# Local and strided attention with a gated feed-forward: scale and identity in the first mask's load, zeros in the values of three units, ScalarE for the last half tile

## The chip, the cores and the metric

One core of a Trainium2 chip. The time is the device time of one execution in microseconds (us); the profile's times count from the first instruction of the profiled execution. PE is TensorE, DVE VectorE, ACT ScalarE, POOL GpSimd, SP SyncE, which issues most DMAs; P V is the product of the attention weights with the values.

## The reference

```python
scores = scale * np.matmul(q, k.transpose(0, 1, 3, 2))        # 8 batches, 8 heads, 576 rows, 64 wide
mask_local = (rel >= 0) & (rel < 32)                          # heads 0 to 3
mask_strided = (rel >= 0) & (pos[None, :] % 32 == pos[:, None] % 32)   # heads 4 to 7
scores = np.where(masks, scores, -1e9); attn = softmax(scores)
x = matmul(attn, v).transpose(0, 2, 1, 3).reshape(4608, 512)
xn = x / sqrt(mean(x * x) + 1e-6) * rms_g                     # the norm, rms_g is its scale
g = xn @ w_gate; val = xn @ w_val                             # 512 x 1536
out = (silu(g) * val) @ w_out                                 # 1536 x 512
```

## The kernel before, in words

Attention is cut into 32 units, one batch and two heads each (numbered from 0; units 0 and 1 of a batch are local heads, 2 and 3 strided ones; the host has put strided heads' rows in residue order, so both kinds are bands). A unit's scores are nine blocks of 64 keys for two halves and two heads. For units 0 to 7 PE first adds the mask by a product with the identity (L744), then the blocks' scores (L759), 36 products of 64 rows by 32 columns. For units 1 to 3 (`PADDED`) the host puts zeros between the two heads in q, so that one product of 128 rows by 64 columns does both heads: 18 products, and q is twice as large. DVE reduces the maxima (L768), ACT takes the exponential (L794, nine small instructions with their sums; for units 2 and 3 PE first subtracts the maximum, L776, and ACT does one pass, L780), DVE divides and transposes, and PE multiplies with the values (L859), 40 products of 32 rows by 64 columns in fp32.

The 4608 tokens are nine chunks of 512. Chunk 0 goes alone: its blocks are squared (L927), summed over rows by PE (L936), scaled by the norm's scale and split into a high and a low part for fp32r products (`convert0`, ACT L992 and DVE L993), then multiplied with the gate and value weights (L1154 and L1164, three products of 128 x 128 x 512 for each block), while the weights, loaded as 64-bit words by SP (L1062), are turned into high and low parts by ACT (L1061, L1066) and DVE (L1069, L625, L1031) and written back to DRAM. The other eight chunks go in pairs by a scheme with seven products for eight (L1308, L1461), with the weights' parts loaded again; the remaining units' attention is set between them.

The order on every engine is made by a planner, `Plan`: each operation is recorded with engine, cost and what it reads and writes; then `forward` places them by a table of due numbers (`DUE`) and some holds. `PLACE` says which of 94 SBUF slots of 128 x 512 each buffer gets, tile names `bl`. So the program's order is fixed before it runs; only semaphores hold an engine. In the opening `LOADS` gives the order of SP's loads: q and k, constants (c0 near mask, c1 strided mask, c2 identity and scale on ACT's queue), v, first weights (w). Four units run in the opening, with filler products on a zero tile (L644) where PE would stand still. At the end each half of the last output tiles is copied from PSUM by ACT and DVE (256 columns each, L623 and L625), and stored (L1549).

Of the kernel before, what the change touches and what calls it, by code (L numbers as in the profile page):

```python
# [25 lines left out]
P = 128  # L26
# [7 lines left out]
MIX = 20  # L34
SWAP = 20
FREE = 5
# [11 lines left out]
NCST = 4 * SW + P  # L48
# [5 lines left out]
PADDED = (1, 2, 3)  # L54
# [21 lines left out]
LOADS = ('q0','c2','c0','q1','c1','q2','v0','q3','v1','w','v2','v3')  # L76
# [7 lines left out]
TLEAD = 2  # L84
PEM = (2,3)
# [9 lines left out]
    "0806003218102404140c0e2c0a5434424f300a003d4d5339221c2152225c55344d3a563e5a282e32001426340818120830202c0a181c1002223b433a"  # L95
    "1400241a5037414b45283032040c2220184636384c5d1c261206593c493b3f142e2c1a28080a044446184a400c00101847504c45481c323006143402"
    "1a5d3b4b5b57282422144e3a44574c0c262c041c2e2006580c0d5d401f4c4a4b1f132a505104342235005859504f032b443f2a145341154338002940"
    "3a3b493139023047584e284c55161a040816060c104842014a563e4b2725191e1f1832484a4d51545237425a1b3746181c205c243e363c264a242c06"
    "143410242d324254164807233d19561a2e085a3e5c461c17013c4a1e04320c244b15193e143352513c0a4d5134205a1c5c17190b070c010e421c322c"
    "1024563c151d07215c4a3d1f2e08523c1504072513154b213c562c340c245a20423533054d0a4a225c321021093415340a223d204d2e240c2c0c4a5a"  # L100
    "4a0d2e420152234b522f2e344442032d3f0813413c215c2700594e2b3d0b25523b120a43243a2a0239580e314c100c0d34402c44473f090f50115513"
    "414f423c532724260149120e432a223d405c004458300825390b2921342d09383c543a53525a38554e41100a4759133e4f483f2831433b51204b3731"
    "23420e00282b0c5c30220d2a11274903434d1e011f1d02561c400844533c5229500f322647355825410b0a3d0959543824395a514c3b12363a10454e"
    "5d5b2146344f485518153e1705421b1a3c431e5306071a1b04401d4d500c144f1d20105517003c1e442f4832233428451f5d13313f4b5515554e575c"
    "42160f3410060e483252533c1946231e375313342b202d1f453a3235293e0157531642574b1a1640452d04075c4d43462b4537054431561e465b293f"
    "1050463e0252080f434b3e5c16501c370e3e1f562350282135483f1a19455318421b133f2035293e460f1f3f081f401e37430e48564d1d4618071b43"
# [12 lines left out]
    "22092354380406580834034e5d365a3f4b43481d0c4c213a3c2911533e2b05072f2c500b3d4f4e0459103135095d254928572a27265b55303248060e"
    "583e0503002b0d2e3c4c0113460f421251194a0402244e390a07385453200c223f362d475d2f5808214b515a433c233a4c051d1924"))  # L120
DUE = np.frombuffer(bytes.fromhex(
    "005a02f60c5a01f801880d2401b30004004e002f03870da7000501a900010000000901f0000600020040025000280035001b0019003700230036001e"
    "001d006c011500aa0122005f00af02c000d100690dac003d0022001a0039002c006601240007012e0d9a024c011d013300da017800a20053004f0101"
    "003b001800030008000a0538009a00b10038004c00120da200a600b5011b01c80da9011402b8009e008e008c0105005c0044004300290011000f01e2"
    "01a605cb0206026504fa0015017e00a401e001a0017c01b6011201e401db007400f9011a01160106010400ef01e5024f00e101d600b000d9014e0263"
    "016102cd01460421025d00bf00e400ad01f700ca00e201d70401034200bd02f400b300c1014c017a022b02de02a2017500e001540266032d02560317"
    "03000319051401e103c401c9025c040f00fe008500ba006200c5007f0076019d002e028402010197017d01dc01d5016b01bf01c30179021b006b02f2"
    "01760237013501ac029301ba023a030102a802430279008100550024002b02f302ec03100153020301ea02180100012b019500b2014501b401be03ee"
    "020f007c00750292015a01eb000b0016000d030b00f5010800bc01e902260264021c01c4029702b7029801c201d30325000c010f014100e301d00152"
    "00d70194025f031c023b01a40182009401cd01a70177018a027d00d601d2007100be039e02e9037402cc021f02fb02e700f20285027c01af016f017f"  # L130
    "00f4013400e9030401df01cc016201bb01fa025902bc028d023100bb00b701cf011e0213032e009f012700c8012f00fa009c006000970367034f0323"
    "010e013e01020186028e028702df02e60163021901a5012c014d019b00d0009b0031001c000e038a019c010d0189023800cf02ba01a201c502d100f7"
    "03320308015101f6033b01e60014008001c1033801a302db023f01f2025502ae02520242020e010c02c1029c01710290026e032a02d3023d022c0283"
    "032002ed039c045003f603bf00d400ed009d015c0086018c004802b202cb026b025800990198010b019102ca02e002e502d90061023902a30267045f"
    "01ad02340343013f028c026d02d0031e0187024d057e021103f2022f016d02c40371027f02270348014401a80275007d022a02720020007e00100235"
    "02dd02320262037a026901650202018f02a70303021d02f001aa0280033c02d202eb02d70251027703e2031502f8026802d502a6035b022d01c00220"
# [332 lines left out]
def attn_moe(ctx: ExitStack, tc: tile.TileContext, qz: bass.AP, qT: bass.AP, kT: bass.AP, vz: bass.AP, vl: bass.AP,  # L469
# [209 lines left out]
    def load_consts(n):  # L679
# [5 lines left out]
        if n != 2:  # L685
            return
# [1028 lines left out]
```

## Time and profile before

| | |
|---|---|
| timed runs | 910.35, 913.11, 917.94 us (median 913.11) |
| the profiled execution | 909.69 us |
| its span, first to last instruction | 907.9 us |
| PE / DVE / ACT busy | 890.1 / 713.0 / 540.3 us |
| DMA, mean over the span | 256 GB/s |

The page divides the span by engine and by line; a group of instructions has its busy time, the mean time of one, and what ended the idle time before it. Matmuls are pipelined, so their records overlap. A released wait is put down to the last semaphore; "issue" means that the profile shows nothing that the engine waited for.

### The profile page before, as it was taken

The numbers are of one execution on the slowest core, as the hardware profiler recorded it, in microseconds if no ns is written. First come the engines' busy times: TensorE is split into PE (matmuls) and PEld (weight loads), VectorE is DVE, ScalarE is ACT, GpSimd is POOL, SyncE is SP. The second block draws the span as 40 slices with busy tenths as digits, with TensorE's granted clock in tenths as the row PEclk, the third lists the DMA queues.
The fourth block names the chain that finished last, engine by engine and source line by source line (L and its number), as shares of the span: only waits on it lengthen the run. The fifth ranks groups of instructions, "written<-read, shape, count | busy, mean of one in ns | idle before, by whom it ended". The sixth has DMA issues, their size and how long they took to land.

```text
span 907.9 us, 21329 instructions
## 1 busy us (share of the span) xinstructions
PE 890.1 (98%) x8570; PEld 718.4 (79%) x8574; DVE 713.0 (79%) x1204; ACT 540.3 (60%) x1154; POOL 1.7 (0%) x14
## 2 busy tenths in 40 slices
PE   7999999999999999999999999999999999999998
PEld 5677788777787877887887888888888888888886
DVE  5889999999888999566779998555699973357972
ACT  5899886688678694455538663444458533334520
POOL 0000000000000000000000000000000000000000
PEclk9999999999999999999999999999999999999999
DMA  9999997999787839957656669655364797353822
GB/s 342 353 411 410 392 414 277 402 410 387 259 318 268 300 116 339 336 165 234 196 175 205 201 204 388 236 157 172 124 206 159 251 359 266 105 163 94 287 97 79
DMA packets 104899, 232.81 MB, mean 256 GB/s; under 512 B 11616, under 2 KB 13920, under 8 KB 102496
## 3 DMA queue, kind: packets, MB, share of 16 engines
q1 hardware_dynamic: 104080, 230.86, 72.5%
q8 instruction: 67, 1.10, 0.5%
q10 hardware_dynamic: 720, 0.59, 0.2%
q14 instruction: 32, 0.26, 0.1%
HBM read 179.51 MB, written 51.90 MB: 255 GB/s over the span
## 4 chain that ended last, share of the span: by engine, by line
PE 85%; DVE 7%; ACT 3%; DMA 3%; issue 2%; ACTq 0%; DVEq 0%
PE a L1308 21%; PE v L1308 13%; PE g L1308 13%; PE a L1461 10%; PE g L1461 6%; PE v L1461 6%; PE a L1209 3%; PE g L1154 3%; PE v L1154 3%; PE pair L750 2%; DVE bl L631 2%; PE pair L846 2%; DMA bl<-gvd 1%; DVE bl L1264 1%; PE a L846 1%
## 5 line engine op out<-in xcount | busy, mean ns | idle before, releaser
L1308 PE MATMUL a<-bl,bl 128*128 128x512 f32 x850 | 215.4, 394 | 0.6 <-DMA bl<-gvd 0.6
L1308 PEld LDWEIGHTS a<-bl,bl 128*128 128x128 f32 x850 | 157.0, 188 | 35.2 <-DVE bl L1481 1.0
L623 ACT CAST bl<-bl 128x512 fp32r<-128x512 f32 (+1 forms) x214 | 130.3, 645 | 75.0 <-DVE bl L1264 24.7
L631 DVE TENSOR_TENSOR bl<-bl,bl 128x512 fp32r<-128x512 f32 x244 | 159.4, 684 | 7.2 <-ACT bl L623 2.7
L1308 PE MATMUL v<-bl,bl 128*128 128x512 f32 x563 | 145.3, 391 | 0.3 <-ACT bl L1316 0.3
L1308 PE MATMUL g<-bl,bl 128*128 128x512 f32 x562 | 144.7, 390 | 0.3 <-DVE bl L1346 0.3
L1264 DVE TENSOR_TENSOR bl<-bl,bl 128x512 f32<-128x512 f32 x169 | 114.0, 684 | 33.7 <-ACT bl L1325 30.7
L1308 PEld LDWEIGHTS v<-bl,bl 128*128 128x128 f32 x563 | 105.2, 188 | 23.9 <-DVE bl L1346 1.1
L1308 PEld LDWEIGHTS g<-bl,bl 128*128 128x128 f32 x562 | 105.1, 188 | 23.1 <-DVE bl L1346 0.8
L1320 DVE TENSOR_TENSOR a<-a,bl 128x512 f32<-128x512 f32 x96 | 66.8, 696 | 70.8 <-PE a L1308 60.4
L1461 PE MATMUL a<-bl,bl 128*128 128x512 f32 x422 | 99.2, 391 | 0.3 <-DVE bl L631 0.3
L1461 PEld LDWEIGHTS a<-bl,bl 128*128 128x128 f32 x422 | 78.9, 188 | 17.3 <-DVE bl L631 0.7
L1461 PE MATMUL g<-bl,bl 128*128 128x512 f32 x279 | 66.9, 390 | 0.0
L1461 PE MATMUL v<-bl,bl 128*128 128x512 f32 x279 | 66.5, 389 | 0.0
L1461 PEld LDWEIGHTS g<-bl,bl 128*128 128x128 f32 x279 | 52.2, 188 | 11.1
L1461 PEld LDWEIGHTS v<-bl,bl 128*128 128x128 f32 x279 | 52.4, 188 | 10.9
L1316 ACT COPY bl<-v 128x512 f32<-128x512 f32 x48 | 28.2, 588 | 50.9 <-PE v L1308 48.3
L1316 ACT COPY bl<-g 128x512 f32<-128x512 f32 x48 | 28.3, 589 | 48.5 <-PE g L1308 48.5
L1325 ACT ACTIVATE bl<-a 128x512 f32<-128x512 f32 x48 | 28.7, 601 | 46.8 <-DVE a L1320 46.7
L1031 DVE TENSOR_TENSOR bl<-bl,bl 128x512 fp32r<-128x512 f32 (+1 forms) x54 | 45.7, 859 | 1.0 <-ACT bl L623 0.9
L1316 ACT COPY bl<-a 128x512 f32<-128x512 f32 x48 | 28.2, 588 | 25.3 <-PE a L1308 22.6
L625 DVE CAST bl<-bl 128x512 fp32r<-128x512 f32 (+1 forms) x84 | 36.5, 444 | 6.8 <-PE v L1308 3.4
(175 smaller groups left out, 1161.2 us busy)
## 6 DMA issues: line engine op xcount, KB each, us to landing
bl<-gvd SPq DMA_DIRECT2D x288, 256.0 KB, 4.6
bl<-od SPq DMA_DIRECT2D x168, 256.0 KB, 3.7
gvd<-bl SPq DMA_DIRECT2D x12, 1024.0 KB, 9.0
bl<-in_wgv_dram SPq DMA_DIRECT2D x11, 1024.0 KB, 11.6
wd<-bl SPq DMA_DIRECT2D x18, 512.0 KB, 9.5
bl<-wd SPq DMA_DIRECT2D x18, 512.0 KB, 7.9
vt<-in_vl_dram SPq DMA_DIRECT2D x24, 352.0 KB, 5.4
xq<-in_qT_dram SPq DMA_DIRECT2D x28, 288.0 KB, 6.3
```

What stands on the lines that cost most here:

```text
L623: nc.scalar.copy(out=o, in_=i)
L625: nc.vector.tensor_copy(out=o, in_=i)
L631: elementwise(CH, lambda e: both(e).tensor_tensor(out=lo.new(F32R), in0=src(), in1=hi.f32(), op=ALU.subtract), reads + [hi.key], [lo.key])
L846: nc.tensor.matmul(out=ends[r % 2][0][n][64 * h:64 * h + 64, at + 32 * lo:at + 32 * hi], lhsT=va()[32 * r:32 * r + 32, D * (6 * n + j):D * ...
L1031: elementwise(len(l) * 256, lambda e, l=l, zs=zs: both(e).tensor_tensor(out=sides(l, 1, F32R), in0=cols(zs), in1=sides(l, 0), op=ALU.subtr ...
L1154: nc.tensor.matmul(out=out_, lhsT=q.t[:, w + at:w + at + P], rhs=x.t, start=(kc == 0 and i == 0), stop=(kc == KC - 1 and i == 2))
L1264: elementwise(CH, lambda e: both(e).tensor_tensor(out=o.new() if fresh else o.t, in0=a.t, in1=b.t, op=how), [a.key, b.key], [o.key])
L1308: nc.tensor.matmul(out=banks[bk], lhsT=w, rhs=xs[k][y].t, start=start and k == 0 and i == 0, stop=stop and k == 1 and i == 2, skip_group_c ...
L1316: op("ACT", act(CH, True), 0, lambda: nc.scalar.copy(out=t.new(), in_=banks[bk]), reads=[bk], writes=[t.key])
L1320: op("DVE", dve(CH), 0, lambda: nc.vector.tensor_tensor(out=banks[bk], in0=banks[bk], in1=t.t, op=ALU.add), reads=[t.key], writes=[bk])
L1325: op("ACT", act(CH, True), 0, lambda: nc.scalar.activation(out=t.new(), in_=banks[bk], func=AF.Silu), reads=[bk], writes=[t.key], tab="silu")
L1461: nc.tensor.matmul(out=banks[bks[j]], lhsT=v, rhs=xs[k][y].t, start=start and k == 0 and i == 0, stop=stop and k == KT - 1 and i == 2, ski ...
```

## The change

- The near mask, the identity and the norm's scale lie side by side in the constants, and one load of SP (c0, 356 words a partition) brings them; the two loads on ACT's queue go. `identb` and `gt` are views of the mask tile `cb`. c0 comes before c2, which is now only the copy of the identity to fp32 on ACT.
- `PADDED` is empty: units 1 to 3 load q once, and take 36 products for their scores.
- `PADV` holds units 1 to 3: the host lays out their values with zeros, twice as large (`vw`), and one product of 64 rows by 128 columns does both heads: 20 products for P V.
- In the last tile's second half both copies are ACT's; the first is stored by SP, the second by ACT.
- `DUE`, `PLACE` and a hold have new values, so the order on all engines and all slots are new. Loads, products and conversions are otherwise the same in number. In the part with the pairs of chunks PE's order stays.

```diff
-PADDED = (1, 2, 3)
+PADDED = ()
-LOADS = ('q0','c2','c0','q1','c1','q2','v0','q3','v1','w','v2','v3')
+LOADS = ('q0','c0','c2','q1','c1','q2','v0','q3','v1','w','v2','v3')
+PADV = (1,2,3)
+PVW = 1350.0
...
-    "0806003218102404140c0e2c0a5434424f300a003d4d5339221c2152225c55344d3a563e5a282e32001426340818120830202c0a181c1002223b433a"
+    "0c321c00081410242006301a563c394b3d0e322843184748222038595840515b27113f4a531c22203408320c2e1412282c180a102e1c162c24393a36"
...
-HOLD_A = [25.0, 0.0, 150.0, 50.0]
+HOLD_A = [25.0,0.0,100.0,50.0]
...
-    cb = sbt([P, 2 * SW], "cb", BF16)
-    identb = sbt([P, P], "identb", BF16)
+    cb = sbt([P, 2 * SW + P + 2 * KC], "cb", BF16)
+    identb = cb[:, 2 * SW:2 * SW + P]
...
-    gt, rcol = few[:, 0:4], few[:, 12:16]
+    gt, rcol = cb[:, 2 * SW + P:].bitcast(F32), few[:, 12:16]
...
-    homes = [(group(4), take2()) for _ in range(NPRO)]
+    homes = [(group(4), group(4) if i in PADV else take2()) for i in range(NPRO)]
...
-        if n == 3:
-            op("SP", 430, 0, lambda: nc.sync.dma_start(out=cb, in_=consts[:, 2 * SW + P:]), writes=["cb", "cb1"], bytes_=P * SW * 4)
-        elif n < 2:
-            op("SP", 430, 0, lambda: nc.sync.dma_start(out=cb[:, SW * n:SW * n + SW], in_=consts[:, SW * n:SW * n + SW]),
-               writes=["cb" + "1" * n], bytes_=P * SW * 2, follow="SP")
+        a, e = ((SW, 2 * SW + P + 2 * KC), (0, SW), (), (0, 2 * SW))[n] or (0, 0)
         if n != 2:
+            at = (n == 3) * (2 * SW + P + 2 * KC)
+            op("SP", 430, 0, lambda: nc.sync.dma_start(out=cb[:, a:e].bitcast(F32), in_=consts[:, (at + a) // 2:(at + e) // 2]), writes=(["cb", "identb", "gt"], ["cb1"], [], ["cb", "cb1"])[n],
+               bytes_=P * (e - a) * 2, run=(1424, 1152, 0, 2304)[n], follow="SP" if n < 3 else None)
             return
-        op("ACT", 430, 0, lambda: nc.scalar.dma_start(out=identb, in_=consts[:, 2 * SW:2 * SW + P]), writes=["identb"], bytes_=P * P * 2, follow="ACT")
-        op("ACT", 430, 0, lambda: nc.scalar.dma_start(out=gt, in_=gain), writes=["gt"], bytes_=2048, follow="ACT")
...
-        n = D * (NBL + 1 if i < EIGHT else NVB)
+        n = D * (NBL + 1 if i < EIGHT else NVB) * (1 + (i in PADV))
...
-        op("SP", 430, 0, lambda: nc.sync.dma_start(out=va(), in_=vz[i] if i < EIGHT else vl[i - EIGHT]), writes=[kv], bytes_=P * n * 4, rel=REL.get(i, 0.0), follow="SP" if pro else None)
+        op("SP", 430, 0, lambda: nc.sync.dma_start(out=va().rearrange("p (a n) -> p a n", a=2), in_=vw[PADV.index(i)].rearrange("a p n -> p a n")) if i in PADV else
+           nc.sync.dma_start(out=va(), in_=vz[i] if i < EIGHT else vl[i - EIGHT]), writes=[kv], bytes_=P * n * 4, run=2560 if i in PADV else 2048, rel=REL.get(i, 0.0), follow="SP" if pro else None)
...
                     for s in range(2):
-                        for h in range(2):
+                        keys = slice(64 * kb - 32 * (kb > 0), min(64 * kb + 32, SW))
+                        if i in PADV:
+                            r = slice(64 * s, 64 * s + 64)
+                            nc.tensor.matmul(out=pr[s][:, 32 * lo:32 * hi], lhsT=va()[r, P * kb:P * kb + P], rhs=pT[r, keys],
+                                             start=kb == 1, stop=kb == NBL - 1, skip_group_check=True)
+                        for h in range(0 if i in PADV else 2):
                             r = 32 * (2 * s + h)
...
-            for n, (e, q) in enumerate((("ACT", nc.scalar), ("DVE", nc.sync))):
+            for n, (e, q) in enumerate((("ACT", nc.scalar), ("DVE", nc.sync)) if more or not j else (("ACT", nc.sync), ("ACT", nc.scalar))):
...
+    vw = np.zeros((max(len(PADV), 1), P, NBL + 1, 2, D), vz.dtype)
+    for n, i in enumerate(PADV):
+        for h in range(2):
+            of = part[part // 32 % 2 == h]
+            vw[n, of, :, h] = vz[i, of].reshape(-1, NBL + 1, D)
```

PE, opening: from the end of unit 0's scores. Before, with `a_85`, `a_86` the banks of unit 1 and `identb` the identity, unit 1's scores:

```order
L744 LDWEIGHTS identb
L744 MATMUL a_85<-cb,identb 128x320
L744 LDWEIGHTS identb
L744 MATMUL a_86<-cb,identb 128x256
L759 MATMUL a_85<-bl_133 64x64 x10
L759 MATMUL a_86<-bl_133 64x64 x8
```

After, two units (line 761 is 759 of before; fillers stand ahead of this piece instead of between the units):

```order
L746 LDWEIGHTS cb
L746 MATMUL a_84<-cb 128x320
L746 LDWEIGHTS cb
L746 MATMUL a_85<-cb 128x256
L761 MATMUL a_84<-bl_137 32x64 x20
L761 MATMUL a_85<-bl_137 32x64 x16
L746 LDWEIGHTS cb
L746 MATMUL a_86<-cb 128x320
L746 LDWEIGHTS cb
L746 MATMUL a_87<-cb 128x256
L761 MATMUL a_86<-bl_145 32x64 x20
L761 MATMUL a_87<-bl_145 32x64 x16
```

Unit 1 and unit 2 have 36 products each now, and follow one another directly.

ACT, opening: before, from unit 1's exponentials, the exponentials of unit 2 (780), the first half weight (1061, 1066) and the copies of unit 0's P V (623), its normed block and square (992, 927):

```order
L794 ACTIVATE pp_70,st_77<-a_85,st_77 128x64 x5
L794 ACTIVATE pp_70,st_77<-a_86,st_77 128x64 x4
L780 ACTIVATE bl_363<-a_87 128x320
L780 ACTIVATE bl_363<-a_88 128x256
L1061 ACTIVATE bl_161<-bl_161 128x512
L1066 ACTIVATE bl_161<-bl_161,few 128x512
L623 COPY bl_129<-g 128x288
L623 COPY bl_129<-v 128x224
L623 COPY bl_417<-v 128x64
L992 ACTIVATE bl_421<-bl_129,few 128x512
```

After (796, 782, 1070, 1075, 627 are 794, 780, 1061, 1066, 623 of before):

```order
L796 ACTIVATE pp_70,st_76<-a_84,st_76 128x64 x5
L796 ACTIVATE pp_70,st_76<-a_85,st_76 128x64 x4
L1070 ACTIVATE bl_158<-bl_158 128x512
L1075 ACTIVATE bl_158<-bl_158,few 128x512
L1070 ACTIVATE bl_158<-bl_158 128x512
L1075 ACTIVATE bl_158<-bl_158,few 128x512
L782 ACTIVATE bl_128<-a_86 128x320
L782 ACTIVATE bl_128<-a_87 128x256
L782 ACTIVATE bl_158<-pair 128x576
L627 CAST bl_484<-bl_429 128x2x256
L627 COPY bl_511<-g 128x288
L627 COPY bl_511<-v 128x224
```

Both half weights come ahead of the exponentials of units 2 and 3 now, and these ahead of unit 0's copies.

SP, opening: before, loads of q (`qz` is q with zeros), constants (in bf16 words), k and v:

```order
L675 DMA bl_129<-in_qT_dram 128x576
L683 DMA cb<-in_consts_dram 128x576
L675 DMA bl_133<-in_qz_dram 128x2x576
L677 DMA bl_133<-in_kT_dram 128x576
L683 DMA cb<-in_consts_dram 128x576
L675 DMA bl_138<-in_qz_dram 128x2x576
L677 DMA bl_138<-in_kT_dram 128x576
L700 DMA bl_155<-in_vz_dram 128x640
L675 DMA bl_141<-in_qz_dram 128x2x576
L677 DMA bl_141<-in_kT_dram 128x576
L700 DMA bl_159<-in_vz_dram 128x640
```

After (`vw` is v with zeros, the constants' words are fp32):

```order
L679 DMA bl_128<-in_qT_dram 128x576
L687 DMA cb<-in_consts_dram 128x356
L679 DMA bl_137<-in_qT_dram 128x576
L681 DMA bl_137<-in_kT_dram 128x576
L687 DMA cb<-in_consts_dram 128x288
L679 DMA bl_145<-in_qT_dram 128x576
L681 DMA bl_145<-in_kT_dram 128x576
L702 DMA bl_152<-in_vz_dram 128x640
L679 DMA bl_131<-in_qT_dram 128x576
L681 DMA bl_131<-in_kT_dram 128x576
L701 DMA bl_156<-in_vw_dram 128x2x640
L1071 DMA bl_158<-in_wgv_dram 128x1024 x2
```

The q loads are half as long, the strided mask stands ahead of unit 2's q as before, and v with zeros stands after unit 3's k; the first weights follow it.

## Rows read from the trace of the kernel before

**Rows 1.** The page, section 1: busy us, share of the span, instructions, by engine.

```profile
PE 890.1 (98%) x8570; PEld 718.4 (79%) x8574; DVE 713.0 (79%) x1204; ACT 540.3 (60%) x1154; POOL 1.7 (0%) x14
```

**Rows 2.** Windows (us): busy us by engine, instructions, then granted clock, DMA share, GB/s.

```profile
core 0: us, PE busy (x) PEld busy (x) DVE busy (x) ACT busy (x) POOL busy (x), PEclk, DMA share, GB/s
0.00:60.00 60.00, 50.94 (x1009) 37.22 (x1014) 44.52 (x90) 46.55 (x141) 1.17 (x12) 1.00 0.98 363
10.00:20.00 10.00, 7.58 (x168) 5.64 (x166) 8.00 (x18) 7.04 (x36) 0.56 (x2) 1.00 1.04 399
40.00:120.00 80.00, 75.45 (x1267) 59.45 (x1267) 74.04 (x140) 77.03 (x200) 0.24 (x1) 1.00 1.03 403
80.00:120.00 40.00, 38.17 (x606) 30.15 (x605) 38.08 (x72) 37.24 (x103) 0.24 (x1) 1.00 1.02 401
890.00:907.90 17.90, 13.83 (x62) 11.11 (x60) 2.23 (x4) 0.74 (x2) 0.00 (x0) 1.00 0.19 65
```

**Rows 3.** Groups of the first 60 us: a filler; count, busy us, mean ns, idle before.

```profile
L644 PE MATMUL a<-still 128*128 128x512 bf16 x8 | 2.4, 380 | 1.1 <-ACT bl L623 0.9 <-issue 0.2
```

**Rows 4.** Timeline of PE: start, us, line, tiles, count, [idle before it and releaser].

```profile
12.12 1.27 PE L759 MATMUL a<-bl 128*64 128x64 f32 x36 [1.00 <-DMA bl<-in_kT_dram]
...
18.52 0.27 PE L859 MATMUL g<-pT,bl 32*64 32x64 f32 x2 [1.07 <-issue]
...
24.86 1.20 PE L859 MATMUL a<-bl,bl 32*64 32x64 f32 x66 [0.69 <-issue]
...
50.51 1.20 PE L759 MATMUL pair<-xk,xq 64*32 64x64 f32 x71
...
53.63 0.24 PE L759 MATMUL pair<-xk,xq 64*32 64x64 f32 x1 [1.91 <-issue]
```

**Rows 5.** The page, section 3, instruction queue: packets, MB, share of 16 engines.

```profile
q8 instruction: 67, 1.10, 0.5%
```

**Rows 6.** The same queue in windows 9.50 to 9.75 and 22.25 to 22.50.

```profile
q8 instruction: 1, 0.02, 25.5%
...
q8 instruction: 1, 0.02, 26.0%
```

**Rows 7.** DMA in the critical chain's opening (start, us), then SP's issues.

```profile
1.64 6.15 DMA few<-in_gain_dram
...
7.80 7.26 DMA bl<-in_kT_dram
...
5.88 0.68 SPq L675 DMA_DIRECT2D bl<-in_qz_dram  x1
...
19.75 0.38 SPq L1062 DMA_DIRECT2D bl<-in_wgv_dram  x1
...
24.82 0.38 SPq L1062 DMA_DIRECT2D bl<-in_wo_dram  x1
```

**Rows 8.** Timeline of ACT in the opening.

```profile
11.27 0.36 ACT L794 ACTIVATE pp<-a,st 128x64 f32<-128x64 f32 x1
...
13.79 0.31 ACT L794 ACTIVATION_READ_ACCUMULATOR pp<-a,st 128x1 f32 x1
...
17.20 0.67 ACT L1061 ACTIVATE bl<-bl 128x512 f32<-128x512 f32 x1 [1.97 <-DMA bl<-in_wgv_dram]
...
17.77 0.73 ACT L1066 ACTIVATE bl<-bl,few 128x512 uint32<-128x512 uint8 x1
...
26.06 1.20 ACT L623 COPY bl<-a 128x256 f32<-128x256 f32 x4 [1.95 <-PE a L859]
...
31.48 0.72 ACT L992 ACTIVATE bl<-bl,few 128x512 fp32r<-128x512 f32 x1
```

**Rows 9.** Timeline of PE: unit 3's P V products.

```profile
28.57 1.39 PE L859 MATMUL pair<-bl,bl 32*64 32x64 f32 x80
```

**Rows 10.** Timeline of the end: the last half tile.

```profile
903.87 0.37 ACT L623 COPY bl<-v 128x256 f32<-128x256 f32 x1 [3.66 <-PE v L1461]
904.27 0.42 DVE L625 COPY bl<-v 128x256 f32<-128x256 f32 x1 [3.61 <-ACT bl L623]
```

More of the change, by code (lines that the diff above doesn't have):

```diff
@@ L468, in attn_moe @@
 @with_exitstack
-def attn_moe(ctx: ExitStack, tc: tile.TileContext, qz: bass.AP, qT: bass.AP, kT: bass.AP, vz: bass.AP, vl: bass.AP,
-             wgv: bass.AP, wo: bass.AP, gain: bass.AP, consts: bass.AP, out: bass.AP):
+def attn_moe(ctx: ExitStack, tc: tile.TileContext, qz: bass.AP, qT: bass.AP, kT: bass.AP, vz: bass.AP, vw: bass.AP, vl: bass.AP,
+             wgv: bass.AP, wo: bass.AP, consts: bass.AP, out: bass.AP):
     nc = tc.nc
@@ L929, in fn @@
                 both(e).tensor_tensor(out=sq.new(), in0=rt.t, in1=rt.t, op=ALU.mult)
-        op("ACT", act(CH), 0, fn, reads=[rt.key], writes=[sq.key], also=way("i", ("DVE", dve(CH), True)))
+        if c == 0 and p in SQP:
+            op("Pool", pool(CH), 0, lambda: fn("Pool"), reads=[rt.key], writes=[sq.key])
+        else:
+            op("ACT", act(CH), 0, fn, reads=[rt.key], writes=[sq.key], also=way("i", ("DVE", dve(CH), True)))
         if c == 0 and SUMPE:
@@ L1548, in pair_of_chunks @@
                 op(e, act(256, True) if e == "ACT" else dve(256), 0, half, reads=[P2[j]] + [dst.key] * (not lead), writes=[("oh", c, j, n)] + [dst.key] * lead)
-                op("ACT" if n == 0 and not more else "SP", 600 if n == 0 else 430, 0, lambda sl=sl, dst=dst, q=q, j=j: (nc.sync if more else q).dma_start(
+                op("ACT" if q is nc.scalar and not more else "SP", 600 if n == 0 else 430, 0, lambda sl=sl, dst=dst, q=q, j=j: (nc.sync if more else q).dma_start(
                     out=outT[P * j:P * j + P, CH + sl.start:CH + sl.stop], in_=dst.t[:, sl]), reads=[("oh", c, j, n), dst.key], bytes_=P * DM * 2)
@@ L1681, in _layout @@
     wo = np.ascontiguousarray(np.asarray(inputs["moe_w_out"]).reshape(NU, P, DM)).view(np.int64)
+    wgv = np.ascontiguousarray(wgv.reshape(NU, 2, P, WCUT, DM // WCUT).swapaxes(2, 3)).reshape(NU, 2 * WCUT, P, DM // WCUT)
+    wo = np.ascontiguousarray(wo.reshape(NU, P, WCUT, DM // WCUT).swapaxes(1, 2)).reshape(NU * WCUT, P, DM // WCUT)
     gain = np.ascontiguousarray(np.asarray(inputs["moe_rms_g"]).reshape(KC, P).T)
     cs = np.zeros((P, NCST), mybir.dt.np(BF16))
[L1685 removed]
+    for z, first in ((0, start), (2 * SW + P + 2 * KC, at8[:, 0])):
         qi = (first[:, None] + 32 * np.arange(NBL)[None, :])[:, :, None]
@@ L1689, in _layout @@
         same = (ki <= qi) & (ki // NROW == qi // NROW) & (ki >= 0)
-        cs[:, z:z + SW] = np.where(near, 0.0, NEG).reshape(P, SW)
-        cs[:, z + SW:z + 2 * SW] = np.where(same, 0.0, NEG).reshape(P, SW)
+        cs[:, z + SW:z + 2 * SW] = np.where(near, 0.0, NEG).reshape(P, SW)
+        cs[:, z:z + SW] = np.where(same, 0.0, NEG).reshape(P, SW)
     cs[:, 2 * SW:2 * SW + P] = np.eye(P)
-    return [("qz", qz), ("qT", qT), ("kT", tr(k)), ("vz", vz), ("vl", vl), ("wgv", wgv), ("wo", wo), ("gain", gain),
+    cs = cs.view(f)
+    cs[:, (2 * SW + P) // 2:(2 * SW + P) // 2 + KC] = gain
+    return [("qz", qz), ("qT", qT), ("kT", tr(k)), ("vz", vz), ("vw", vw), ("vl", vl), ("wgv", wgv), ("wo", wo),
             ("consts", cs)]
```

315 lines of the change are left out of this document (158 added, 157 removed).

## The prediction

> **What bounds the kernel now.** The page's busy times come first: TensorE (PE) is busy 890.1 of 907.9 us, no other engine over 79% [rows 1]. PE idles 17.8 us in all, so a gain has little to come from. The windows by stage say where those lie: 9.06 us in the first 60, 1.83 between 80 and 120, 4.07 in the last 17.9; the other 790 us idle 2.9 [rows 2]. The granted clock there is 1.00, which is 2.4 GHz. The change is at the two ends: the opening and the last copies; the long serial part keeps its PE order. In the opening PE also runs 18 filler products that count as busy; eight of them are 2.4 us [rows 3], so all some 5. So some 14 us lie in the opening, and a part of that (the first 5 us, before data is in) cannot go.
>
> Then the timeline of PE, for what ends its idle time. Three waits have nothing behind them that the profile shows ("issue"): 1.07 us at 18.52, 0.69 at 24.86, 1.91 at 53.63 [rows 4]. Counted in the printed order (an fp32 product is four instructions, two loads and two matmuls; fp32r or bf16 is two), they stand at instructions 700, 954 and 1970 of PE: 254 apart, and four times 254. The instruction queue moves 67 packets of 16 KB, and 17,144 PE instructions make 256 to each [rows 1, 5]; packets start at 9.5 and 22.25 us [rows 6], the second 2.6 us before the wait ends at 24.86. So PE's program comes in pieces of about 254, and the next piece but one is asked for when PE enters one: entered at 18.52, the piece after is usable at 24.86, 6.3 us later. Large products hide this; the small ones of attention don't. The first such border, 446, was crossed just after 12.12 and shows no wait of its own [rows 4]; the packet of 9.5 plus 2.6 gives 12.1, so it was just there.
>
> Rule against row: the Trainium skill, "Runtime: NRT & Kernel Launch", section "Instruction fetch mechanics", says that the program is refilled in 16 KiB blocks of 256 instructions and that this is mostly hidden. The block agrees with the 256 to a packet, the hiding not with the three waits. By that rule the opening would go as fast as its loads: rival 2.
>
> Last the DMA issues and ScalarE (ACT). The 2 KB load of the scale lands after 6.15 us, at 7.79; only then unit 3's k is issued (7.80, the q before it at 5.88), and it lands at 15.06 [rows 7]. ACT starts the fourth normed block (L992) at 31.48 [rows 8], and from 40 to 120 us ACT is busy 77.03 of 80 us, PE 75.45: ACT is as full as PE there [rows 2].
>
> **The change part by part.** *Loads.* Scale and identity ride in the near mask's load, so two ACT loads go, and with them the hold before unit 3's k. The q of units 1 to 3 halve (3 x 288 KB less), their v double (3 x 320 KB more, all but one behind the first weights). Up to unit 3's k that is 3,810 KB before and 2,950 after; at 0.40 MB/us [rows 2] the 860 KB are 2.2 us, the bandwidth lost in the hold some 0.7 more. So unit 3's k lands near 12 us, and the first weights (taken at 17.20 [rows 8]) near 15. In total 0.1 MB more: 0.2 us, beside a PE that is not waiting for loads.
>
> *Products.* Unpadded scores of units 1 to 3 are 36 products instead of 18 each: 72 PE instructions more a unit, ahead of all P V. Their P V falls from 40 products to 20: 80 instructions less each, but later. The trace has no product of 64 x 128. Nearest rows: padded scores (128 rows by 64 columns) 1.27 us for 36 matmuls, 35 ns each; unpadded ones 1.20 us for 71, 17 ns [rows 4]; P V 1.39 us for 80 [rows 9]. So a unit's 40 matmuls take 0.7 to 1.4 us against 1.39: -0.7 to 0 each. I take 0, the row with the wide tile; PE waits for its program there anyway, so the low end also gives little.
>
> The Trainium skill, "TensorEngine Tiling (Array Packing)", section "Tiling Modes", has eight parallel tiles of 32x64 but two of 64x128; by that, half the matmuls on a quarter of the tiles take twice 1.39 us. The rows differ: from eight tiles (64x32) to two (128x64) a matmul went from 17 to 35 ns, not to 68. By the rule unit 3's P V would end 1.4 us later: rival 4.
>
> *Where the borders fall now.* 446 falls into unit 1's scores, 700 into unit 3's, 954 near the end of unit 0's P V, 1208 into unit 3's. The first late piece is asked for in unit 0's scores (instruction 192, 5.8 us), which moves little, so I put it at 11.9. Bounds: the step from request to use was 6.2 (12.3 to 18.52) and 6.3 us under full DMA; after 24.86 the next border (1208, in the P V at 28.57 [rows 9]) shows no wait, so 3.7 can do; and it can be a us longer: 9.5 to 13. The next borders follow at 6.2 each: 18.1, 24.3, 30.5.
>
> *The chain through the opening, after.* Unit 1's scores end at 12.6, reduce and scaling 0.7: 13.3. Its exps take 2.8 (11.27 to 14.1 [rows 8]): 16.1. Two half weights follow on ACT at 1.3 (17.20 to 18.50): 18.7. Unit 3's scores wait for 18.1 and end at 19.0, lowering 19.7, two exps (0.8 + 0.6) 21.1. But unit 0's P V ends at 24.6. Units 0 and 1 cost ACT 1.4 each (copies 0.7, L992 0.7): 27.4; a square 0.5, unit 2 1.9 (copies 1.2 [rows 8]), a square 0.5: 30.3. Unit 3's P V ends at 30.8, its copies take 1.2: the fourth block starts at 32.0 against 31.48. **+0.5 us**: what the loads gain is given back to the fetch.
>
> *What follows.* Border 1970, 1.91 us in unit 6's scores, now falls into weight products (some 0.23 us each) of the third gate block. From the border before it lie 0.5 us of P V, 1.5 of scores and 12 products, 2.7: 4.7 us of PE work against a step of 6.2. So 1.5 is left of the wait at most: **-0.4**, up to -1.9 if those products wait for their weights anyway. ACT goes on with one exp table load more (1.28) and one full weight (L1061 and L1066, 2.2) less done than before at this point: 3.5 us late in a stretch where it idles 3.0 [rows 2]. Before the products that use them PE has its own work in a row, and by my count the second and third weights come when it gets there: I take 0, bound 3.5.
>
> *End.* The last half tile is copied by VectorE at 904.27 to 904.69, only after ScalarE's half [rows 10]. ScalarE needs 0.37 where VectorE needs 0.42 and signals no other engine: **-0.1**; at worst its second copy and the store's issue queue up, +0.3.
>
> Sum: +0.5 - 0.4 + 0 - 0.1 = **0.0 us** on the profiled execution of 909.69 us (1.8 around its span). The timed runs are 910.35, 913.11 and 917.94, so this execution is 3.4 under their median. The middle of all four is 911.7, and from that I forecast **911.7 us**. What a measurement can tell from no change here is about 1%, 9 us; this is far inside.
>
> **Rivals.**
> 1. *The first piece is there at 9.5.* The borders follow at 15.7, 21.9 and 28.1, and unit 3's P V ends 2.4 us earlier: fourth block at 29.6, 1.9 ahead. With the whole 1.9 of border 1970, sum -1.9 - 1.9 - 0.1 = -3.9: 907.8. For it: fewer tiny packets lie ahead of it (the scale's go). Against: two steps of 6.2 to 6.3 under the same full DMA.
> 2. *The fetch is hidden* and the opening follows its loads: weights 15.1, halves 17.7, exps 19.1, units 0 to 2 and two squares 24.8, unit 3's P V and copies 28. That is 3.4 ahead, and 908.2 with the end. Against: three waits, each at a border.
> 3. *ACT becomes the bound, and the kernel is slower.* Place: 40 to 120 us. The extra table load and the weight put back reach PE as waits for weights, and a PE that waits keeps nothing of border 1970. It decides from the point where ACT's lateness exceeds what PE has in a row: +0.5 + 3.5 - 0.1 = +3.9: 915.6. For it: ACT's 77.03 of 80. Against: PE idles only 1.83 from 80 on, with DVE and ACT as full.
> 4. *The wide P V takes twice as long*: +1.4: 913.1.
> 5. *SP's queue holds back weights.* Slots are handed out anew everywhere. Before, SP stood from 20.1 to 24.82 at one load [rows 7], 4.7 us; in the long part such a stand stops PE. Two give +9.4: 921.1, three are over 1%.
>
> **How the numbers follow.** Forecast 0.56, rival 1 0.22, rival 2 0.02, rival 3 0.12, rival 4 0.04, rival 5 0.04. The likeliest one's bounds: low -1.9 and -0.1 give 909.7, high 1.1 more for a piece at 13 and 0.3 at the end 913.1. Rivals 1 and 3 widen this to 907.8 and 915.6; the runs shown lie up to 3.4 under and 4.8 over their median, so I add 3.3 below and 2.4 above: 904.5 to 918. Faster by over 1% (below 904.0) needs rival 1 and a low set of runs: 0.04. Slower by over 1% (above 922.2) needs rival 5 three times: 0.04. Within 1%: 0.92.
>
> **What would show it.** Right: an "issue" wait of PE in unit 1's scores that ends near 12 us, one in unit 3's near 18, one at the end of unit 0's P V near 24; none in unit 6's scores and under 1.6 in the third gate block; the fourth norm block on ACT starting at 31 to 33 us; unit 3's k landed by 13; P V of units 1 to 3 at 0.7 to 1.4 us. Rival 1: the first of these waits ends before 10. Rival 3: PE waits for ACT, or for VectorE behind it, between 40 and 120. Wrong altogether: PE idle of over 3 us in any stage after 120 us, or a time outside the range.

## The result and the profile after

The changed kernel takes **918.93 us** (median of 20 executions, 910.55 to 922.58); the kernel before, run beside it, 910.82. The ratio is **1.0068, 95% interval 1.0047 to 1.0088**: slower, by less than 1%. The ratio is worked out from undisturbed executions (two of the 20 of before took 1099.61 and 1215.49 us) and is not the quotient of the two medians, which is 1.0089. Forecast were 911.7 us and a range of 904.5 to 918.0; the median lies 0.9 us above the range.

The 20 executions are two groups. Where TensorE's mean granted clock is 0.997 or 0.998 of 2.4 GHz (5 executions) they take 910.55 to 912.83 us; where it is 0.984 to 0.991 (15), 916.13 to 922.58. Nothing lies between. The trace that comes with the result (911.82 us) is of the first group, so it shows the opening but hardly the loss:

```profile
PE 894.0 (98%) x8562; PEld 722.4 (79%) x8566; DVE 714.9 (79%) x1211; ACT 535.6 (59%) x1143; POOL 3.4 (0%) x18
```

Windows by stage, the columns as in [rows 2]:

```profile
0.00:60.00 60.00, 51.65 (x994) 38.78 (x999) 39.27 (x79) 44.69 (x137) 2.18 (x13) 1.00 0.97 359
40.00:120.00 80.00, 75.31 (x1260) 58.82 (x1259) 71.51 (x135) 73.62 (x190) 0.74 (x3) 0.98 0.99 377
120.00:890.00 770.00, 768.74 (x6525) 625.95 (x6525) 617.94 (x1025) 436.20 (x869) 0.76 (x3) 1.00 0.71 243
```

PE idles 16.0 us where it idled 17.8 [rows 1], but is busy 3.9 longer; three times 1.06 us of that are the P V of units 1 to 3. The timeline of PE answers to [rows 4, 9]:

```profile
10.83 0.55 PE L761 MATMUL a<-bl 64*32 64x64 f32 x25 [1.32 <-issue]
...
16.98 0.98 PE L761 MATMUL pair<-bl 64*32 64x64 f32 x55 [1.42 <-issue]
...
23.05 0.27 PE L866 MATMUL v<-pT,bl 32*64 32x64 f32 x1 [1.44 <-issue]
...
23.48 2.45 PE L862 MATMUL a<-pT,bl 64*128 64x64 f32 x40
...
29.96 2.45 PE L862 MATMUL pair<-bl,bl 64*128 64x64 f32 x40
...
52.51 0.41 PE L746 MATMUL pair<-cb 128*128 128x320 bf16 x2 [2.12 <-ACT bl L627]
...
80.93 0.32 PE L752 MATMUL pair<-xk,xq 64*32 64x64 f32 x8 [1.49 <-issue]
```

Three waits at the borders of PE's program stand in the three places that were named, each 1.1 to 1.3 us earlier than forecast; a unit's wide P V takes 2.45 us and not 1.39. ACT's timeline gives what follows, against [rows 8, 10]: the first weight, the fourth normed block, the two last half copies (x2).

```profile
15.40 0.67 ACT L1070 ACTIVATE bl<-bl 128x512 f32<-128x512 f32 x1 [0.45 <-DMA bl<-in_wgv_dram]
...
33.63 0.72 ACT L1001 ACTIVATE bl<-bl,cb 128x512 fp32r<-128x512 f32 x1
...
906.11 0.65 ACT L627 COPY bl<-v 128x256 f32<-128x256 f32 x2 [3.71 <-PE v L1470]
```

In this trace the clock fell once ahead of the end, after the wait that ends at 80.93, to 1.2 GHz for 3.4 us (windows of 4 us):

```profile
80.00:84.00 4.00, 3.07 (x15) 2.41 (x16) 2.69 (x4) 3.97 (x5) 0.00 (x0) 0.69 1.02 413
84.00:88.00 4.00, 4.00 (x72) 3.08 (x74) 2.64 (x6) 3.06 (x18) 0.25 (x1) 0.88 1.03 409
```

### The profile page after: what moved, and what is told of

Its sections match the earlier page's. It is cut to its first block, busy times and chain, and to the rows that moved or that the text cites. A ratio compares the mean times of both kernels' runs of the same rounds, so it can differ in the third digit from the quotient of the medians.

```text
span 910.0 us, 21348 instructions
## 1 busy us (share of the span) xinstructions
PE 894.0 (98%) x8562; PEld 722.4 (79%) x8566; DVE 714.9 (79%) x1211; ACT 535.6 (59%) x1143; POOL 3.4 (0%) x18
## 4 chain that ended last, share of the span: by engine, by line
PE 89%; ACT 6%; DMA 2%; DVE 1%; issue 1%; SPq 0%; ACTq 0%
PE a L1317 22%; PE g L1317 15%; PE v L1317 14%; PE a L1470 11%; PE g L1470 7%; PE v L1470 7%; PE pair L752 2%; PE g L1163 2%; PE a L1218 2%; PE pair L848 2%; PE v L1163 2%; ACT bl L1075 1%; ACT pp L796 1%; PE a L848 1%; ACT pp L810 1%
## 5 line engine op out<-in xcount | busy, mean ns | idle before, releaser
L627 ACT CAST bl<-bl 128x512 fp32r<-128x512 f32 (+1 forms) x208 | 125.9, 642 | 72.3 <-DVE bl L1273 31.0
L1317 PE MATMUL g<-bl,bl 128*128 128x512 f32 x573 | 146.7, 391 | 0.1
L1273 DVE TENSOR_TENSOR bl<-bl,bl 128x512 f32<-128x512 f32 x165 | 111.1, 685 | 33.6 <-ACT bl L1334 32.2
L1317 PEld LDWEIGHTS g<-bl,bl 128*128 128x128 f32 x573 | 106.9, 188 | 24.3 <-DVE bl L1355 1.0
L1470 PE MATMUL g<-bl,bl 128*128 128x512 f32 x286 | 68.0, 390 | 0.0
L1470 PEld LDWEIGHTS g<-bl,bl 128*128 128x128 f32 x286 | 53.5, 188 | 11.3
L629 DVE CAST bl<-bl 128x512 fp32r<-128x512 f32 (+1 forms) x90 | 39.4, 446 | 6.5 <-PE g L1317 1.9
```

What stands on the lines that cost most here:

```text
L627: nc.scalar.copy(out=o, in_=i)
L629: nc.vector.tensor_copy(out=o, in_=i)
L1273: elementwise(CH, lambda e: both(e).tensor_tensor(out=o.new() if fresh else o.t, in0=a.t, in1=b.t, op=how), [a.key, b.key], [o.key])
L1317: nc.tensor.matmul(out=banks[bk], lhsT=w, rhs=xs[k][y].t, start=start and k == 0 and i == 0, stop=stop and k == 1 and i == 2, skip_group_c ...
L1470: nc.tensor.matmul(out=banks[bks[j]], lhsT=v, rhs=xs[k][y].t, start=start and k == 0 and i == 0, stop=stop and k == KT - 1 and i == 2, ski ...
```

## The experiments

Two theories. *Clock*: the loss is time in which PE runs at 1.2 GHz. *Path*: the wide P V, or the new order, is longer at any clock.

**Both kernels once more** (`b0` is before, `a0` the changed kernel; no edit).

> The kernel before, once more, for the granted clock of its executions. Clock theory (the changed kernel loses its time where TensorE's granted clock falls from 2.4 to 1.2 GHz; its 20 executions lie in two groups, 910.6 to 912.8 us at a mean clock of 0.997 or 0.998, and 916.1 to 922.6 us at 0.984 to 0.991): most executions of the kernel before stand at 0.997 or more, and those above 914 us at less. Rival, a longer path in the opening (products of 64 rows by 128 columns at 2.45 us a unit against 1.39): the clocks of the two kernels are spread alike, and the changed one is longer at every clock.

> The changed kernel, once more, for a second trace and its clocks. Clock theory: again two groups, most executions at 0.984 to 0.991 and 916 us or more; if the profiled one is of that group, its windows show PE's clock at 1.2 GHz for a stretch of 13 to 29 us (0.008 to 0.016 of 910 us, doubled) and elsewhere the same times as the first trace. Rival (path): 919 at any clock.

Before: 912.44 us (ratio to its other executions 1.0009 [0.9996, 1.0023]), mean clock 0.994 to 0.998, only 2 of the 12 at 0.997 or more, where I had expected most. After: 919.44 us (1.0081 [1.0046, 1.0115]), six executions of seven at 0.984 to 0.991, as expected. The trace of this second run of the changed kernel fell into the slower group. Its PE timeline in the opening:

```profile
23.12 0.27 PE L866 MATMUL v<-pT,bl 32*64 32x64 f32 x1 [1.71 <-issue]
...
23.55 3.47 PE L862 MATMUL a<-pT,bl 64*128 64x64 f32 x40
...
27.67 4.53 PE L862 MATMUL a<-bl,bl 64*128 64x64 f32 x40
...
34.57 4.53 PE L862 MATMUL pair<-bl,bl 64*128 64x64 f32 x40
```

and two windows of it:

```profile
24.00:32.00 8.00, 8.00 (x77) 7.45 (x75) 4.38 (x7) 2.94 (x9) 0.00 (x0) 0.55 0.98 360
32.00:44.00 12.00, 12.00 (x126) 8.60 (x127) 2.36 (x4) 7.23 (x14) 0.00 (x0) 0.59 0.38 127
```

After the wait of 1.71 us the clock falls near 25 and comes back near 42: 17.1 us at 1.2 GHz, in which PE never idles. (It also falls twice for 3.4 us, at 11.1 and 89.6; the trace above has one such fall, near 81.) The same products are slower by up to 1.85 times (4.53 against 2.45 us), unit 3's P V ends at 39.1 instead of 32.4, and the span is 917.5 instead of 910.0. So 6.7 of the 7.5 us between the two executions of one program arise here. The Trainium skill, "TensorE: Matmul & The Clock Gate", section "What's actually happening", says that activity releases the throttle. The row speaks against it in this form: busy 8.00 of 8 and 12.00 of 12 us, and the clock stays down.

The trace of `b0` lost clock too, 6.8 us from 19.1 us on. It fell during a wait in unit 0's P V, which had taken 1.07 us in [rows 4]:

```profile
20.66 0.37 PE L859 MATMUL g<-pT,bl 32*64 32x64 f32 x2 [3.81 <-issue]
```

Over the 144 executions of before in this section (`b0` and those beside the other runs) the mean clock's median is 0.995, and 3 of them are at 0.991 or less, against 21 of 27 of the changed kernel, whose median is 0.989. **At 0.997 and 0.998 the two kernels are alike: 911.19 us (33 executions of before) and 911.35 (6).** At 0.9995 and more before takes 906.1 to 908.4 us (5 executions; its profiled one, at 1.00 too, took 909.69). The changed kernel never got there, so what its path costs at full clock is not shown. An estimate from the two median clocks, with the work taken as twice as long at 1.2 GHz: 0.006 of some 915 us, 5.5 us, is the clock's part. The gap is 6.2 us by the ratio and 8.1 by the medians; the rest stays open.

**The last half tile by VectorE again** (`tail`).

```diff
-(("ACT", nc.scalar), ("DVE", nc.sync)) if more or not j else (("ACT", nc.sync), ("ACT", nc.scalar))
+(("ACT", nc.scalar), ("DVE", nc.sync))
```

> The changed kernel with the last half tile copied by VectorE again and stored by SP. Both theories: within 0.5 us of the changed kernel at the same clock; the end 0.1 us later. The clocks stay in two groups.

917.24 us, 1.0065 [1.0039, 1.009]; 9 of 12 at 0.991 or less: no different from the changed kernel. Its trace repeats that of `a0`: after a wait of 1.71 us the clock falls at 26.0, for 17.1 us.

**Wide or narrow P V, unpadded or padded scores.** Narrow is

```diff
-    nc.tensor.matmul(out=pr[s][:, 32 * lo:32 * hi], lhsT=va()[r, P * kb:P * kb + P], rhs=pT[r, keys], ...
+    for h in range(2):
+        r = 32 * (2 * s + h)
+        w = P * kb + D * h
+        nc.tensor.matmul(out=pr[s][64 * h:64 * h + 64, 32 * lo:32 * hi], lhsT=va()[r:r + 32, w:w + D], rhs=pT[r:r + 32, keys], ...
```

in units 1 to 3 (`narrow`; `u3`: in unit 3 alone); padded is `PADDED = (1, 2, 3)` again with q's zeros (`pad`; `padnarrow` has both). The order on all engines is kept.

> The changed kernel with the P V of units 1 to 3 as 40 products of 32 rows by 64 columns again (the same loads with zeros). Path theory: P V of a unit back from 2.45 to 1.39 us, three times 1.06: 3 us faster, about 916. Clock theory: PE has 3 us less to do in the opening but the waits at the borders of the program's pieces move (80 more instructions a unit), so the two groups stay if the clock falls later than the opening, at the wait that ends near 81 us, and the median stays within 2 us of 919; if the mean clock is back at 0.997 or more, the median is 911.

> The changed kernel with the scores of units 1 to 3 padded again, 18 products instead of 36 a unit, q with zeros loaded (864 KB more, 2.2 us of loading), order the same; the wide P V stays. It tells which part of the change brings the waits. If the 216 instructions of the unpadded scores are what moved a border to the end of unit 0's P V: the issue waits in unit 1's and unit 3's scores and there go or move, the clock falls in fewer executions, median 911 to 915. If the wide P V alone is the cause: two groups again, 917 to 920.

> The changed kernel with padded scores and the P V of units 1 to 3 as 40 products of 32 rows by 64 columns: of the change the loads (scale and identity in the mask's load, values with zeros), the tables and the tail remain. Theory: instructions and products as in the kernel before, so its clock too (0.994 to 0.998), and a time of 911 to 914; if the new order on ScalarE costs anything by itself, it shows here as more than 914 at a clock of 0.996 or more.

> The changed kernel with unit 3's P V alone as 40 products of 32 rows by 64 columns. Clock theory: where the clock falls near 25 us it stays down through the wide P V of units 1 and 2 and comes back in unit 3's, near 35 us: some 10 us at 1.2 GHz against 17.1 with three wide ones and 6.8 with none; median 915.5 to 917.5. Path theory: 1.06 us less: 918.

| scores, P V of units 1 to 3 | us | ratio to before |
|---|---|---|
| unpadded, wide (the changed kernel) | 918.93, 919.44 | 1.0068 [1.0047, 1.0088], 1.0081 [1.0046, 1.0115] |
| unpadded, narrow (`narrow`) | 914.07 | 1.0031 [1.0012, 1.0051] |
| unpadded, wide in two units (`u3`) | 915.57 | 1.0035 [1.0017, 1.0054] |
| padded, wide (`pad`) | 917.76 | 1.0050 [1.0027, 1.0074] |
| padded, narrow (`padnarrow`) | 912.53 | 1.0007 [0.9990, 1.0024] |

The wide P V costs some 5 us with unpadded and 5.2 with padded scores. With unpadded scores it takes 1.2 (wide) and 1.5 us (narrow) longer than with padded ones, which the intervals don't separate. Loads, constants and the new order alone (last line) show no cost in time, though the mean clock there is 0.990 to 0.996 and not the 0.994 to 0.998 that I had expected. So the 216 instructions of the scores, the cause in one of the expectations, are at most the smaller part. 914.07 us for `narrow` is what neither theory had (916, or 917 to 921, or 911).

It is not the 1.06 us a unit that decides. With narrow P V the products are 3.2 us shorter in all, but PE has 240 instructions more and stands at two further borders in the opening, 2.1 us together:

```profile
27.94 1.75 PE L863 MATMUL a<-bl,bl 32*64 32x64 f32 x52 [0.93 <-issue]
...
34.40 0.34 PE L863 MATMUL pair<-bl,bl 32*64 32x64 f32 x7 [1.19 <-issue]
```

The three executions of this kernel at 0.998 take 912.0 to 913.0 us, no less than the changed one at that clock. What differs is how long the clock stays down; the mean clock's median is 0.994, against 0.989. In the trace with narrow P V it falls at the same place, near 25 us, and is back at 31.7, with the first of the two waits in between:

```profile
24.00:32.00 8.00, 6.79 (x150) 4.47 (x142) 5.03 (x8) 5.29 (x15) 0.00 (x0) 0.57 0.98 376
32.00:44.00 12.00, 10.81 (x205) 7.52 (x209) 6.40 (x13) 8.81 (x27) 0.00 (x0) 1.00 0.77 271
```

6.8 us at 1.2 GHz against 17.1. With unit 3 alone narrow it was 13.7 us (I had expected 10); with padded scores and wide P V 10.2, where it fell later, in unit 2's. These are one trace each.

**Large products between the wide ones** (`mix`). Fillers (zeros, 128 x 128 x 512) ahead of the P V of units 2 and 3:

```diff
         def values():
             pT = pT_()
+            if i in (2, 3):
+                fill(6, pr[1])
```

> The changed kernel with six large filler products (zeros, 128 x 128 x 512) ahead of the wide P V of unit 2 and of unit 3, 1.3 us each at 2.4 GHz. The wait before unit 0's P V ends stays, so the clock should still fall near 25 us in most executions. If it is the wide P V that keeps it at 1.2 GHz, the large products between bring it back sooner: 6.8 to 10.3 us at 1.2 GHz instead of 17.1, median 915 to 918 (3.5 to 5 us won, 2.6 given to the fillers). If the clock stays down for a fixed time or for another reason: 17.1 us again and 921 to 922.

918.50 us, 1.0066 [1.0044, 1.0087]. In the trace the clock falls at 24.5, where it fell in `a0`, and is back at 31.4, within the first six fillers; unit 2's P V then takes 2.45 us again:

```profile
24.36 4.39 PE L864 MATMUL a<-pT,bl 64*128 64x64 f32 x40
...
29.27 2.51 PE L648 MATMUL a<-still 128*128 128x512 bf16 x6
31.71 2.45 PE L864 MATMUL a<-bl,bl 64*128 64x64 f32 x40
```

6.8 us instead of 17.1, so it is what PE does, not only that it is busy. In time nothing was won, and the median is just above the 915 to 918 expected: the fillers take 2.6 us at full clock, and in this trace the clock fell again for 6.8 us at 58.7, during a wait of 2.1 us for ACT's copies, and for 3.4 at 120.

**The wait covered** (`cover`). Fillers where PE stood:

```diff
         def values():
             pT = pT_()
+            if i == 0:
+                fill(7, pr[1])
```

`bcover` is the same edit in the kernel before; `cover3` adds seven ahead of unit 1's scores and two fp32 products of 512 columns ahead of unit 8's.

> The changed kernel with seven filler products (zeros, 0.21 us each) ahead of unit 0's P V, where PE otherwise stands still for 1.4 to 1.7 us before 23 us. Clock theory (the fall at 25 us follows that wait, and the wide P V keeps PE at 1.2 GHz for 17 us): the wait ends at the same time but is under 0.5 us, no fall at 25 us, the group at 916 to 922 us goes, median 911.5 to 913. Path theory (the wide P V alone costs the time): PE has no less to do, 919 as before.

> The kernel before with the same seven fillers ahead of unit 0's P V (where it waited 1.1 us in one trace, 3.8 in the other, and the clock fell in the second only, for 6.8 us). Clock theory: the fall near 19 us comes in fewer executions; median 1 to 3 us below the kernel before. If the fall has another cause: within 0.5 us, or 1.5 us slower as PE does that much more.

> As the one before, with seven fillers ahead of unit 1's scores too (wait of 1.3 to 2.3 us that ends near 10.5) and two fp32 products of 512 columns, 1.9 us, ahead of unit 8's scores (wait of 1.5 us that ends near 81). Clock theory: no fall in the first 100 us, mean clock 0.998 or more in nearly all executions, 910 to 911.5; if that holds it is at or under the kernel before (912.2 in the runs beside). Path theory: 919 and more, since PE gets 5 us more to do.

`cover`: **911.21 us, 0.9990 [0.9980, 0.9999]**, no execution of 12 under 0.996. The same program with 1.5 us more work on PE is some 7 us faster (0.9990 against 1.0068 of before). Its trace has the fillers, 0.3 us left of the wait, and wide P V at 2.45 us throughout:

```profile
20.76 2.10 PE L648 MATMUL v<-still 128*128 128x512 bf16 x9
...
24.16 0.27 PE L868 MATMUL g<-pT,bl 32*64 32x64 f32 x2 [0.31 <-issue]
...
24.66 2.45 PE L864 MATMUL a<-pT,bl 64*128 64x64 f32 x40
```

This is the run that the path theory can't have. `cover` ran on another chip than `a0`; `u3`, beside it on that chip, kept its loss (1.0035, clocks 0.988 to 0.993), so the chip isn't the reason. At 0.9995 and more two executions of `cover` take 910.2 and 910.5, 2 to 4 us above before's five. Three times 1.06 would fit that, but two executions of a program with seven fillers more don't show it. `bcover`: 911.56, 0.9995 [0.9978, 1.0013], no difference shown, where 1 to 3 us were expected; in its trace 2.2 us of the wait were left and the clock fell for 6.8 us. `cover3` missed: 913.82, 1.003 [1.0009, 1.0051]. The clock held better (median 0.997), but at 0.997 and more it takes 913.6, some 2.5 us above the others at that clock. Its trace has a wait of 2.3 us in a later unit's P V; that this and the added work are the reason was not tested.

**Fewer instructions ahead.**

```diff
-FIRST = (44, 6)
+FIRST = (8, 9)
```

`slim` and `bslim` keep the order; `slimp` lets it be worked out anew.

> The changed kernel with 36 of the 44 small products on zeros at the very start replaced by three large ones: 138 instructions fewer ahead of everything, order and work otherwise the same. Theory (PE's program comes in pieces of 254 that are asked for one ahead and take some 6.2 us; the waits at the borders bring the clock down): the borders stand 138 instructions later in the work; the waits in unit 1's scores (1.3 to 2.3 us) and unit 3's go, unit 0's P V isn't interrupted, one wait of at most 1.7 us is left in unit 2's P V near 24 us; unit 3's P V ends 1.5 to 2 us earlier. Clock at 0.996 or more in most executions, median 909 to 912. If the waits have nothing to do with the number of instructions: they stay where they are, 919.

> The kernel before with the same edit at the start. Its first waits (border 446 and 700) move later; the border that was at the start of unit 0's P V then stands in unit 1's, where a wait of 1 to 3 us stays. Theory: median 909 to 912 against 912.2, more executions at 0.998 or more; if it stays at 912 to 913, the wait left in the P V decides for that kernel.

> The same, with the order on all engines worked out anew for the smaller count, which also leaves out 15 of the fillers in the opening. Theory: as the one before, within 2 us of it.

`slim`: 911.58 us, 0.9994 [0.9974, 1.0014], 907.49 at the lowest. The waits moved with the count: unit 0's P V is not interrupted, unit 2's scores are, instead of unit 1's.

```profile
12.29 0.65 PE L761 MATMUL a<-bl 64*32 64x64 f32 x30 [2.05 <-issue]
```

The clock still fell near 25 us in this trace, for 6.8 us, after a wait of 0.56 in unit 2's P V:

```profile
24.56 3.44 PE L862 MATMUL a<-bl,bl 64*128 64x64 f32 x31 [0.56 <-issue]
...
30.37 3.06 PE L862 MATMUL pair<-bl,bl 64*128 64x64 f32 x40
```

It came back within unit 3's wide P V, so wide products don't always keep it down. `bslim`: 911.97, 0.9997 [0.9984, 1.0009]: a wait of 2.4 us stayed in unit 1's P V, and nothing was gained. `slimp` missed widely, 948.26 us, 1.0401 [1.0377, 1.0424]: the due numbers fit one set of costs, and with the other count the order on VectorE and ScalarE changed in hundreds of rows. The first line of PE's waits:

```profile
PE pair L848 <- DVE pT L827: 7.6, 1, 7.6
```

**Waits and clock together.** `slimfill`: `slim` with the nine fillers ahead of unit 3's scores moved ahead of unit 2's, and four more ahead of unit 0's P V; `both` leaves the nine where they were and puts five ahead of unit 2's.

> The changed kernel with the shorter start (36 small products less, three large ones more), the nine fillers ahead of unit 3's scores moved ahead of unit 2's, where that run waited 2.1 us for its program, and four fillers more ahead of unit 0's P V, so that the border in unit 2's P V (wait of 0.6 us at 24.6, then 6.8 us at 1.2 GHz) is reached later. Clock theory: no fall in the first 100 us in most executions, mean clock 0.997 or more, median 907.5 to 909.5, below both kernels. If the clock falls for the products of P V and not for the waits: again 6.8 us or more at 1.2 GHz near 25 us, 911 to 914.

> The changed kernel with the shorter start, five fillers ahead of unit 2's scores, the nine ahead of unit 3's scores kept (in slimfill their move left a wait of 1.9 us for VectorE), and four more ahead of unit 0's P V. Clock theory: the opening goes without a fall, waits of 1 us or less, unit 3's P V ends near 31 us; the falls near 52 (after a wait of 2.1 us for ScalarE's copies) and near 113 us may come: 908.5 to 910.5, at or under slimfill and 0.2 to 0.4% under the kernel before. Rival (more fillers only delay): 911 to 913.

`slimfill`: **910.54 us, 0.9986 [0.9971, 1.0001]**, the lowest median of all, some 7 us below the changed kernel; against before no difference is shown, and 907.5 to 909.5 at a clock of 0.997 was expected (measured 0.996). Its trace has no fall in the opening, one near 52 after PE waited 2.2 us for ACT's copies (ahead of unit 6's scores, as at 52.51 above) and one near 113. Unit 3's lowering, the product that subtracts the maximum, waits for VectorE:

```profile
18.54 1.24 PE L782 MATMUL pair<-st,ident 128*128 128x320 f32 x4 [1.91 <-DVE st L774]
```

`both`: 911.59, 0.9986 [0.9969, 1.0003], which the rival had (911 to 913) and not the clock theory. Its trace is one of the two of 12 at 0.991 or less, and the one that limits the theory:

```profile
24.85 3.26 PE L868 MATMUL a<-bl,bl 64*128 64x64 f32 x40 [0.34 <-issue]
...
30.47 4.53 PE L868 MATMUL pair<-bl,bl 64*128 64x64 f32 x40
```

No wait of more than 0.73 us stands ahead, yet the clock fell near 26, after some 6 us of P V with one large product, and stayed down 13.7 us. `slim` above, and `pad` (fall at 26.4), are like it:

```profile
24.41 2.77 PE L862 MATMUL a<-bl,bl 64*128 64x64 f32 x40 [0.71 <-DVE bl L827]
```

So a long wait just ahead isn't needed for a fall near 25 us. Executions at 0.991 or less are rarer where the waits were covered or moved: 21 of 27 of the changed kernel, 4, 0 and 2 of 12 of `slim`, `slimfill` and `both`, 0 of 12 of `cover`. But `pad`, whose trace has no wait over 0.9 us between 8 and 26 us, has 5 of 10. That a wait makes a fall more frequent is likely by these counts, not shown.

## Why the prediction was wrong

1. *What bounds it, the pieces of 254, the borders.* Right. The waits came where they were put, at 10.83, 16.98 and 23.05 for 11.9, 18.1 and 24.3, and the first lies inside 9.5 to 13 (10.5 in `a0`, 11.3 in `cover`). The second is not steady: 1.42 us here, 0.27 in `cover`, none in `a0`. So it isn't only semaphores that hold an engine; PE also waits for its own program. Rival 2, the fetch that the Trainium skill calls mostly hidden ("Runtime: NRT & Kernel Launch", section "Instruction fetch mechanics"), didn't come about: the three waits are 1.32 to 1.44 us.
2. *Loads.* Right. Unit 3's k, issued at 5.34, landed 7.1 us later at 12.4 (forecast near 12), and the first weight was taken at 15.40 (near 15). The gain was given back to the fetch, as foreseen.
3. *"So a unit's 40 matmuls take 0.7 to 1.4 us against 1.39 ... I take 0."* **This step failed first.** They take 2.45 us, 1.06 more a unit and outside both bounds. Rival 4, at 0.04, had the size. Its twice 1.39, 2.78 us, is an estimate from the eight and two parallel tiles of the Trainium skill ("TensorEngine Tiling (Array Packing)", section "Tiling Modes"). The padded scores misled: from 64 rows by 32 columns to 128 by 64 a matmul goes from 17 to 35 ns [rows 4], but from 32 by 64 to 64 by 128 from 17 to 61 (2.45 us by 40). The fourth normed block started 2.15 us late, at 33.63, and not 0.5.
4. *"The granted clock there is 1.00, which is 2.4 GHz."* **This is the step that cost the 8 us between the two groups.** The prediction read one execution of before that had this clock, as only 5 of the 144 do; no term, no rival and no bound let it change. In 21 of 27 executions of the changed kernel the mean clock is 0.991 or less. Where a trace shows such an execution (`a0`, and `tail`, which differs at the end alone), PE is at 1.2 GHz for 17.1 us from near 25 us on, through the wide P V. That the loss goes with the clock is shown by `a0` against the first trace and by `cover`; that the wide P V has part in it, by the table and by `mix`. Which waits bring a fall, and why it also comes without a long one, is open.
5. *Border 1970, -0.4.* This term failed too. The wait of 1.91 us at that border went, but PE now stands 2.12 us for ACT's copies at 52.51, ahead of the same unit 6's scores: nothing was won.
6. *ACT 3.5 us late: "I take 0".* Not right at that one place: ACT's weight conversions, until 51.9, stand ahead of these copies, which is the sign that was named for rival 3. The wait, 2.1 us, is in all 13 traces with the change's order and in none of the four with before's, and in seven of the 13 the clock falls in it or within 1.5 us after it. In time it takes the place of the 1.91 us, and `padnarrow`, which has it, is no slower than before. Otherwise ACT is no fuller than it was, 73.62 of 80 us [rows 2]. Rival 5 didn't come: from 120 to 890 us PE idles 1.3.
7. *End, -0.1.* Within noise (`tail`).
8. *The range.* It was built from four times of before and the sum's bounds; a lower clock was not in it. Above, it adds 2.4 us, though one of the four lies 4.8 over their median.

That the first group of executions, 910.55 to 912.83 us, lies at the 911.7 of the forecast is partly luck: its trace has 3.2 us of P V that the sum did not have.

## What to carry to other kernels

Read the granted clock of several executions, not of one trace, before taking PE's rates as fixed: here a wait of 1.71 us in front of small tiles was followed by a loss of 6.7 us in one execution, and one of 1.44 us by none in another. Half as many matmuls need not be less time: at 128 rows by 64 columns they took 35 ns each, at 64 by 128 they took 61. Compare a tile with rows of the same number of rows and columns, and if there are none, let the range hold twice the old time. Where PE waits for its own program, large products on zeros in the wait's place can win: some 7 us for seven of them in `cover`. The same seven in the kernel before won nothing that shows, and more of them (`cover3`) lost 2.6 us against `cover`.

## What was not expected of the hardware

- In `a0` PE, busy without a gap, stayed at 1.2 GHz for 17.1 us on fp32 products of 64 rows by 128 columns with 32 or 64 moving columns, with one to three products of 128 x 128 x 512 between the units. In `mix` it was back at 2.4 GHz within six of these in a row.
- The same border's wait differed by 2.7 us between executions of one program (1.07 and 3.81 us in before and `b0`); the clock fell in the second only.
